# An attention and feed-forward kernel on one core: the third chunk's opening steps are placed earlier, and four coarse pieces change their places

## The chip, the cores and the metric

The kernel runs on one core of a Trainium2 chip. The metric is the device time of one execution in microseconds (us); lower is better. The kernel before took 1090.92 us, the median of three runs (1090.62 to 1091.01).

## The reference

The reference computes two attentions over the same q, k, v (8 batches, 8 heads, 576 positions, 64 values each) and adds them; then an RMS norm and a gated feed-forward layer over the 4608 tokens.

```python
# coarse: q, k, v are averaged over groups of 4 positions, attended in full, repeated 4 times
q_d = q.reshape(B, H, Sd, factor, D).mean(axis=3)          # Sd = 144; k_d and v_d likewise
out_up = np.repeat(sm_attn(q_d, k_d, v_d), factor, axis=2)
# local: each position sees the positions less than 4 away (7 of them)
mask = np.abs(pos[:, None] - pos[None, :]) < factor
scores = np.where(mask, scale * np.matmul(q, k.transpose(0, 1, 3, 2)), -1e9)
out_local = np.matmul(softmax(scores), v)
x = (out_up + out_local).transpose(0, 2, 1, 3).reshape(4608, 512)
# feed-forward: 512 -> 1536 (gate and value) -> 512
xn = x / np.sqrt(np.mean(x * x, axis=-1, keepdims=True) + 1e-06) * rms_g
g = xn @ w_gate
return (g * (1 / (1 + np.exp(-g))) * (xn @ w_val)) @ w_out
```

## The kernel before

**Tiles and loops.** The 4608 tokens are 18 chunks of 256 columns. The feed-forward layer of a chunk runs over 12 tiles f of 128 hidden columns. For each tile TensorE computes gate and value (`first`, L1334, 24 matmuls into `ps_h`, twelve with `wg` and twelve with `wv`); ScalarE takes the tanh (L1342); VectorE makes the gate (L1345) and the product (L1350); ScalarE and VectorE split that into a high and a low part (L1356, L1359); and two tiles later TensorE adds the tile to the output (`second`, L1370, 6 matmuls). There are three `ps_h` buffers, so a tile's first matmul waits for the product (L1350) of the tile three before it. The lag of two tiles is LAG; at a chunk's end its last seconds run behind the next chunk's first tiles. Below, f8 is tile 8 of chunk 1, and f0', f3' are tiles of chunk 2.

**The coarse attention** is done in pieces, one for a batch and a pair of heads. A piece has three TensorE steps: scores (L529), the turn of its exponentials (L569), and the values (L584). Between scores and turn VectorE takes the peak (L550, L555), and ScalarE the exponentials (L560); after the turn ScalarE copies (L577), and after the values VectorE scales (L598) and a DMA stores the rows in `up_dram` (L601). The sums of k, q and v over groups of four, which a piece needs, are made by DMAs: one load on SyncE's queue (L359, L363) and three accumulating ones on GpSimd's queue (L367).

**The local attention of most chunks** runs while the chunk before it is in its feed-forward layer, on VectorE (L706 products, L710 sums: 8 of each for a chunk), and for the weighted values on ScalarE (L753, eight small instructions for a product), VectorE and GpSimd (L760), summed on VectorE (L779); then the coarse rows are added (L795), the squares taken (L805), and the chunk is normed and transposed to `xh` and `xl` (two buffers each). Its k and v rows come in `kv` buffers (four; L612, on SyncE's queue), its q rows in `q_t` (two; L694).

**The first three chunks** take another way for it, class `Dense`: scores on TensorE with a mask, then `flip` (L1149, TensorE transposes the shares of a parity), `copy` (L1160, ScalarE), `values` (L1172, 64 instructions here, from four `kv` buffers and the two `prod` buffers with the shares), `load_up` (L1196, two DMAs on ScalarE's queue, which bring the coarse rows), `add_rows` (L1201, adds these to the same accumulators; its second operand is called `q_t` in the profile because it lies in the place of such a buffer), `squares` (L1214), `rms` and `root` (L1223 to L1238, very small VectorE instructions), `norm`, `turn` (L1256), `high` (L1260) and `low` (L1264).

**What sets the order.** Every engine takes its instructions in the program's order. The weight decoding, `Dense(0)`, `Dense(1)`, the scores and softmax of `Dense(2)`, and all of chunk 0's feed-forward layer are ordered by a planner (class `Plan`): each step has a cost, a due time, and the buffers that it takes and holds. This part is called the list. From chunk 1 on the steps are written in a loop over the tiles; there a table says behind which step a piece goes:

```python
for at, it in zip(PIECES.get(c, (0, 3)), coarse[done:]):
    score, swap, value = Coarse(*it).steps()
    behind_second[at] = score
    before.setdefault(at + 2, []).append(swap)
    before.setdefault(at + 3, []).append(value)
```

So a coarse piece at 5 has its scores behind the second that is written at tile 5, its turn behind tile 7, its values behind tile 8. A framework's scheduler puts what is written so into each engine's order; a step can move some places from where it was written. In the same way the remaining steps of `Dense(2)` are given places among chunk 1's tiles: `flips` at tile 1, `mix` (values, add_rows, squares, rms and root) at tile 3, `turn` at tile 6. Chunk 3's local attention, the first in the vector form, is written in chunk 2's loop, and the scheduler has moved it forward: in the trace its L706 to L779 run while TensorE is in chunk 1.

## Time and profile before

| | |
|---|---|
| runs | 1090.92, 1091.01, 1090.62 us; median 1090.92 |
| the profiled execution | 1090.25 us, of which span 1088.4 us |
| TensorE (PE) busy | 1042.2 us, 96% |
| VectorE (DVE) busy | 889.0 us, 82% |
| ScalarE (ACT) busy | 602.3 us, 55% |
| GpSimd (POOL) busy | 207.1 us, 19% |
| PE's share of the chain that ended last | 85% |

All times of the trace are counted from the start of the span. Chunk 1's first tile ends and its f1 begins at 150.5 us; chunk 2's f3' begins at 227.6 us. In the timeline a row is a run of equal instructions on one engine: start, time, line, what is written from what, the count, and in brackets the idle time ahead of it with what ended it. In a table of windows each row is a stretch of time: its length, then the busy time and count of PE, PEld, DVE, ACT and POOL, the granted clock of TensorE (1.00 is full), the share of the DMA engines, and GB/s.

### The profile page before, as it was taken

What the parts mean: (1) busy time and instruction counts of PE and PEld (TensorE: products, weight loads), DVE (VectorE), ACT (ScalarE), POOL (GpSimd) and SP (SyncE); (2) the same over time, 40 slices, a digit from 0 to 9 for tenths busy, and PEclk for the clock granted to TensorE, in tenths of its full rate; (3) what the DMA queues carried; (4) which work ended last, traced back from release to release, by engine and by line L of the source; (5) the groups of instructions that cost most, each with busy time, mean ns of one, the idle gap of its engine ahead of it and who ended that gap; (6) DMA issues with size and microseconds to landing.
All of it is one profiled execution on the core that took longest, in us unless ns stands there. A gap on an engine that the chain in (4) does not pass through costs nothing.

```text
span 1088.4 us, 23630 instructions
## 1 busy us (share of the span) xinstructions
PE 1042.2 (96%) x8804; PEld 956.6 (88%) x8804; DVE 889.0 (82%) x1855; ACT 602.3 (55%) x2182; POOL 207.1 (19%) x268
## 2 busy tenths in 40 slices
PE   4878898899999999999999999999999999999998
PEld 3657797799999999999999999999999999999997
DVE  5899847894979998898988889989898998986432
ACT  5587641843748383838374747373838373746222
POOL 2257600322222122121121212010101010101000
PEclk9989999999999999999999999999999999999999
DMA  8598814474352535253535353313132232210000
GB/s 265 190 325 236 211 49 124 95 172 91 105 116 74 121 96 127 83 122 82 123 87 126 81 119 83 89 50 96 46 99 71 71 91 64 84 37 21 1 21 20
DMA packets 72729, 113.26 MB, mean 104 GB/s; under 512 B 26006, under 2 KB 33958, under 8 KB 72614
## 3 DMA queue, kind: packets, MB, share of 16 engines
q1 hardware_dynamic: 46342, 91.64, 27.9%
q0 software_dynamic: 8768, 15.95, 9.5%
q10 hardware_dynamic: 17504, 4.16, 1.8%
q8 instruction: 69, 1.13, 0.4%
q14 instruction: 46, 0.38, 0.1%
HBM read 99.92 MB, written 11.80 MB: 103 GB/s over the span
## 4 chain that ended last, share of the span: by engine, by line
PE 85%; DVE 7%; ACT 3%; DMA 2%; issue 2%; POOL 0%; SPq 0%; ACTq 0%; DVEq 0%; POOLq 0%
PE ps_h L1334 51%; PE ps_o L1370 26%; PE ps_a L584 2%; PE ps_a L529 1%; DVE o_sb L275 1%; PE ps_a L856 1%; PE ps_a L569 1%; DMA wv<-in_qk_sum_dram 1%; ACT prod L753 1%; ACT a_g L560 1%; DVE prod L706 1%; DMA qk<-in_qk_sum_dram 1%; DMA q_t<-in_q_band_dram 0%; PE ps_h L1101 0%; PE ps_a L1149 0%
## 5 line engine op out<-in xcount | busy, mean ns | idle before, releaser
L1370 PE MATMUL ps_o<-wo,hs 128*128 128x512 f32 x1296 | 335.8, 397 | 2.0 <-DVE hs L1359 2.0
L1334 PE MATMUL ps_h<-xh,wg 128*128 128x256 f32 x1728 | 317.2, 279 | 0.6 <-DVE wg L299 0.6
L1334 PE MATMUL ps_h<-xh,wv 128*128 128x256 f32 x1728 | 312.2, 278 | 0.0
L1334 PEld LDWEIGHTS ps_h<-xh,wg 128*128 128x128 f32 x1728 | 266.2, 189 | 9.2 <-issue 3.1
L1334 PEld LDWEIGHTS ps_h<-xh,wv 128*128 128x128 f32 x1728 | 264.7, 188 | 3.2 <-issue 0.6
L1370 PEld LDWEIGHTS ps_o<-wo,hs 128*128 128x128 f32 x1296 | 229.0, 188 | 40.7 <-DVE hs L1359 2.4
L753 ACT ACTIVATE prod<-kv,sc 128x64 f32<-128x64 f32 x960 | 245.3, 407 | 21.2 <-DMA up<-o_g 10.3
L1334 PE MATMUL ps_h<-xl,wg 128*128 128x256 f32 x864 | 244.0, 282 | 7.3 <-DVE sil L1350 5.7
L1334 PE MATMUL ps_h<-xl,wv 128*128 128x256 f32 x864 | 240.3, 278 | 4.3 <-DVE sil L1345 4.3
L1342 ACT ACTIVATE sil<-ps_h 128x256 f32<-128x256 f32 x216 | 81.7, 378 | 241.3 <-PE ps_h L1334 223.5
L1334 PEld LDWEIGHTS ps_h<-xl,wg 128*128 128x128 f32 x864 | 163.2, 189 | 15.1 <-DVE sil L1350 7.2
L1334 PEld LDWEIGHTS ps_h<-xl,wv 128*128 128x128 f32 x864 | 162.9, 188 | 7.5 <-DVE sil L1345 6.2
L760 POOL TENSOR_TENSOR prod<-sc,kv 128x256 f32<-128x256 f32 x120 | 89.2, 775 | 407.2 <-DVE sc L744 152.8
L1356 ACT ACTIVATE hs<-sil 128x256 fp32r<-128x256 f32 x216 | 89.4, 414 | 126.4 <-DVE sil L1350 105.3
L779 DVE TENSOR_REDUCE x_t<-prod 128x128 f32<-128x896 f32 x120 | 127.8, 1075 | 29.6 <-PE ps_a L856 26.4
L1345 DVE SCALAR_TENSOR_TENSOR sil<-sil,ps_h 128x256 f32<-128x256 f32 x216 | 88.9, 411 | 58.7 <-ACT sil L1342 56.1
L706 DVE TENSOR_TENSOR prod<-q_t,kv 128x896 f32<-128x896 f32 x120 | 129.5, 1082 | 5.6 <-DMA kv<-in_k_pad_dram 4.5
L710 DVE TENSOR_REDUCE sc<-prod 128x14 f32<-128x896 f32 x120 | 128.6, 1073 | 0.0
L1359 DVE TENSOR_TENSOR hs<-sil,hs 128x256 fp32r<-128x256 f32 x210 | 100.3, 479 | 31.2 <-ACT hs L1356 30.7
L1350 DVE SCALAR_TENSOR_TENSOR sil<-sil,ps_h 128x256 f32<-128x256 f32 x216 | 89.6, 416 | 3.0 <-PE ps_h L1334 1.5
L367 POOL DMA_DIRECT2D qk<-in_qk_sum_dram x36 | 32.9, 913 | 233.5 <-DMA qk<-in_qk_sum_dram 195.5
L760 DVE TENSOR_TENSOR prod<-sc,kv 128x128 f32<-128x128 f32 x120 | 52.5, 461 | 0.8
(182 smaller groups left out, 927.9 us busy)
## 6 DMA issues: line engine op xcount, KB each, us to landing
kv<-in_k_pad_dram SPq DMA_DIRECT2D x60, 320.0 KB
kv<-in_v_pad_dram SPq DMA_DIRECT2D x60, 320.0 KB
qk<-in_qk_sum_dram POOLq DMA_DIRECT2D x36, 288.0 KB, 4.8
q_t<-in_q_band_dram SPq DMA_DIRECT2D x60, 128.0 KB
out_dram<-o_sb SPq DMA_DIRECT2D x30, 256.0 KB
vs<-in_v_sum_dram POOLq DMA_DIRECT2D x36, 144.0 KB, 3.5
qk<-in_qk_sum_dram SPq DMA_DIRECT2D x12, 288.0 KB
wo<-in_qk_sum_dram SPq DMA_DIRECT2D x2, 1152.0 KB
```

The source lines that it names most:

```text
L706: nc.vector.tensor_tensor(out=pr, in0=bcast(q[:, s0:s0 + 2], 2, NO), in1=window(k, s0), op=ALU.mult)
L710: nc.vector.tensor_reduce(out=self.sc[:, j, par, s0:s0 + 2], in_=self.pr[i], axis=AX.X, op=ALU.add,)
L753: nc.scalar.activation(out=self.pr[i][:, o, s], in_=self.v[j, par][:, s0 + s + o], func=AF.Copy, scale=p[:, s, o:o + 1],)
L760: (nc.vector if engine == "DVE" else nc.gpsimd).tensor_tensor(out=self.pr[i][:, a:b], in0=bcast(p[:, :, a:b].rearrange("p s o -> p o s"), ...
L779: nc.vector.tensor_reduce(out=self.x[j][:, s0:s0 + 2, par], in_=pr.rearrange("p o s d -> p s d o"), axis=AX.X, op=ALU.add,)
L1334: last = nc.tensor.matmul(out=self.p[f][:, t], lhsT=wi(f)[:, 0, k], rhs=xi[:, k], start=(n == 0), stop=(n == 3 * KT - 1),).ins
L1342: nc.scalar.activation(out=self.sil[f], in_=self.p[f][:, 0], func=AF.Tanh, scale=0.5)
L1345: nc.vector.scalar_tensor_tensor(out=self.sil[f], in0=self.sil[f], scalar=1.0, in1=self.p[f][:, 0], op0=ALU.add, op1=ALU.mult,)
L1350: nc.vector.scalar_tensor_tensor(out=self.sil[f], in0=self.sil[f], scalar=0.5, in1=self.p[f][:, 1], op0=ALU.mult, op1=ALU.mult,)
L1356: nc.scalar.activation(out=self.hs[f][:, 0], in_=self.sil[f], func=AF.Copy)
L1359: (nc.gpsimd if engine == "POOL" else nc.vector).tensor_tensor(out=self.hs[f][:, 1], in0=self.sil[f], in1=self.hs[f][:, 0], op=ALU.subtract,)
L1370: last = nc.tensor.matmul(out=self.o[j], lhsT=lhs[:, cols], rhs=rhs(f)[:, 0], start=(f == 0 and i == 0), stop=(f == NF - 1 and i == 2),).ins
```

## The change

It has three parts. (1) The coarse pieces of chunk 1 stand at tiles 1, 4, 6, 8 in place of 0, 5, 7, 8. (2) `Dense(2)`'s two flips, their copies and its `load_up` leave chunk 1 and go into the list; `mix` stands at tile 0 of chunk 1 rather than 3, and `turn` at 3 rather than 6. (3) `load_up` of `Dense(1)` and `Dense(2)` brings the coarse rows into the `xh` buffer that the chunk is to fill later, rather than into a buffer of the weight stage, and no longer stands behind the list's last step. No computation is added or left out. As the planner lays out the list anew, some steps in it change their places too, one weight step goes from VectorE to GpSimd, and a weight load of the stage comes earlier on SyncE's queue.

```diff
-PIECES = {1: (0, 5, 7, 8), 2: (0, 3), 3: (0, 2)}
+PIECES = {1: (1, 4, 6, 8), 2: (0, 3), 3: (0, 2)}
...
 # Dense.plan (chunk 1)
-                up = buf("stage")
                 t = task(
-                    "ACT", 0.1, self.load_up, end - 12, [stored[p.b, p.hp] for p in pieces], allocs=[up], uses=[up], lag=9.0,
-                )
-                ups = [task("PE", 1.6, self.add_rows, end - 12, [t, *values], uses=[up, *x_bufs])]
+                    "ACT", 0.1, self.load_up, end - 12, [stored[p.b, p.hp] for p in pieces], allocs=[self.xh_buf],
+                    uses=[self.xh_buf], lag=9.0,
+                )
+                ups = [task("PE", 1.6, self.add_rows, end - 12, [t, *values], uses=[self.xh_buf, *x_bufs])]
...
-        def plan_scores(self, sums, mask, at, late):
+        def plan_scores(self, sums, pieces, mask, at, late):
...
+            copies = []
             for par in range(2):
-                made = self.plan_softmax(par, late - 5, held[par:par + 1], made, sp[par], s_bufs[par])
+                sb = s_bufs[par]
+                made = self.plan_softmax(par, late - 5, held[par:par + 1], made, sp[par], sb)
+                tp = buf("ps_a")
+                t = task("PE", 1.1, lambda par=par: self.flip(par), late + 8, made, allocs=[tp], uses=[sb, tp])
+                copies.append(task(
+                    "ACT", 0.6, lambda par=par: self.copy(par), late + 8, [t, *copies], uses=[tp, sb],
+                ))
...
+            self.xh_buf = buf("xh")
+            task("ACT", 0.1, self.load_up, late + 20, [stored[p.b, p.hp] for p in pieces], allocs=[self.xh_buf], lag=9.0)
...
 # Dense.steps (chunk 2)
-            return [(0.0, self.load_up)], {1: flips, 3: mix, 6: turn}
+            return [], {0: mix, 3: turn}
...
         def load_up(self):
-            t = stage.tile([P, WPC, 2], U32, name="raw")
-            self.up = t.bitcast(FP32).rearrange("p n t -> p (n t)")[:32]
+            self.xh = xp.tile([P, KT, C], FP32R, name="xh")
+            self.up = self.xh.bitcast(FP32).rearrange("p k n -> p (k n)")[:32]
...
-            with behind(listed and listed[-1]):
```

The order on the engines, at three places. First TensorE around chunk 2's values, at the end of the list and in chunk 1's opening tiles (names: `kv` are the v rows, `prod` the flipped shares, `raw` the coarse rows, `wo` with `hs` a second). Before:

```order
L584 MATMUL ps_a<-vs,a_g 72x64 x8
L1172 MATMUL ps_a<-kv,prod 32x64 x64
L1201 MATMUL ps_a<-raw,q_t 128x256 x4
L1370 MATMUL ps_o<-wo_0_850,hs 128x512 x2
L1370 MATMUL ps_o<-wo_0_851,hs 128x512
```

That is behind f3 of chunk 1; the second that follows is tile 1's. Now:

```order
L1337 MATMUL ps_h<-xh,wv_0_846 128x256
L1175 MATMUL ps_a<-kv,prod 32x64 x18
L1373 MATMUL ps_o<-wo_2_1872,hs 128x512 x2
L1373 MATMUL ps_o<-wo_2_1873,hs 128x512
L1373 MATMUL ps_o<-wo_2_1872,hs 128x512 x2
L1373 MATMUL ps_o<-wo_2_1873,hs 128x512
L1175 MATMUL ps_a<-kv,prod 32x64 x46
L1203 MATMUL ps_a<-xh,q_t 128x256 x4
L1337 MATMUL ps_h<-xl,wg_0_779 128x256
```

The values and the coarse rows now stand behind chunk 1's f0, with chunk 0's last second among them, and ahead of f1; three tiles, two seconds and the first piece's turn and values that stood ahead of them stand behind. (Lines from the first change on count some more: L1337 is L1334 of before, L1373 is L1370, L1175 is L1172, L1203 is L1201.)

Second, TensorE at the second coarse piece of chunk 1, whose scores are L529 and whose turn is L569. Before, from the last transposes of chunk 2 on:

```order
L1256 MATMUL ps_a<-ident_sb,x_t 128x128 x4
L1370 MATMUL ps_o<-wo_0_850,hs 128x512 x2
L1370 MATMUL ps_o<-wo_0_851,hs 128x512
L1370 MATMUL ps_o<-wo_0_850,hs 128x512 x2
L1370 MATMUL ps_o<-wo_0_851,hs 128x512
L569 MATMUL ps_a<-ident_sb,a_g 72x72 x8
```

There the piece's scores lie ahead of that, before 21 matmuls of f11, and the second shown is tile 4's. Now, from its scores on:

```order
L529 MATMUL ps_a<-qk 72x144 x4
L1373 MATMUL ps_o<-wo_0_850,hs 128x512 x2
L1373 MATMUL ps_o<-wo_0_851,hs 128x512
L1373 MATMUL ps_o<-wo_0_850,hs 128x512 x2
L1373 MATMUL ps_o<-wo_0_851,hs 128x512
L1337 MATMUL ps_h<-xl,wv_1_1603 128x256
L1337 MATMUL ps_h<-xh,wv_1_1603 128x256
L1337 MATMUL ps_h<-xh,wv_1_1604 128x256
L1337 MATMUL ps_h<-xl,wv_1_1603 128x256
L1337 MATMUL ps_h<-xh,wv_1_1603 128x256
L1337 MATMUL ps_h<-xh,wv_1_1604 128x256
L569 MATMUL ps_a<-ident_sb,a_g 72x72 x8
```

The second between is tile 3's, and the six matmuls are the last of f9: the turn stands ahead of f10 and f11, which before stood ahead of it.

Third, ScalarE at the same piece, whose exponentials are L560. Before:

```order
L733 ACTIVATE sc<-sc 128x112
L1246 ACTIVATE x_t<-ps_a,rinv 128x256 x2
L1342 ACTIVATE sil<-ps_h 128x256
L753 ACTIVATE prod<-kv,sc 128x64 x16
L1260 CAST xh<-ps_a 128x4x128
L753 ACTIVATE prod<-kv,sc 128x64 x2
L560 ACTIVATE a_g,z_g<-ps_a,m_g 72x144 x4
L753 ACTIVATE prod<-kv,sc 128x64 x12
```

Now:

```order
L733 ACTIVATE sc<-sc 128x112
L1263 CAST xh<-ps_a 128x4x128
L753 ACTIVATE prod<-kv,sc 128x64 x16
L1359 ACTIVATE hs<-sil 128x256
L601 DMA up<-o_g 72x4x64
L1359 ACTIVATE hs<-sil 128x256
L753 ACTIVATE prod<-kv,sc 128x64 x9
L1359 ACTIVATE hs<-sil 128x256
L753 ACTIVATE prod<-kv,sc 128x64 x7
L1345 ACTIVATE sil<-ps_h 128x256 x2
L560 ACTIVATE a_g,z_g<-ps_a,m_g 72x144 x4
```

Between the exponentials of chunk 3's local attention (L733) and those of the coarse piece (L560) stood 18 instructions of L753, and now stand 32, with three high parts (L1359 now) and two tanh (L1345 now).

More of the change, by code (lines that the diff above doesn't have):

```diff
@@ L945, in plan @@
                 turn = task(
-                    "PE", 0.6, lambda b=b: self.turn(b), end - 7 - TAIL, norms,
-                    allocs=[tps] + ([self.xh_buf, self.xl_buf] if b == 0 else []), uses=[xs, self.xh_buf, self.xl_buf],
+                    "PE", 0.6, lambda b=b: self.turn(b), end - 7 - TAIL, [*norms, *self.turns],
+                    allocs=[tps] + ([self.xh_buf, self.xl_buf][not early:] if b == 0 else []), uses=[xs, self.xh_buf, self.xl_buf],
                 )
@@ L1050, in steps @@
         def steps(self):
-            def flips():
-                last = [self.flip(par) for par in range(2)][-1]
-                for par in range(2):
-                    self.copy(par)
-                return last
             def mix():
@@ L1190, in load_up @@
         def load_up(self):
-            t = stage.tile([P, WPC, 2], U32, name="raw")
-            self.up = t.bitcast(FP32).rearrange("p n t -> p (n t)")[:32]
+            self.xh = xp.tile([P, KT, C], FP32R, name="xh")
+            self.up = self.xh.bitcast(FP32).rearrange("p k n -> p (k n)")[:32]
             src = up_dram[0].rearrange("b k t (s g) d -> s g (b k t) d", g=UPP)[:, self.u0:self.u0 + 2]
-            with behind(listed and listed[-1]):
-                for g in range(2):
-                    nc.scalar.dma_start(out=self.up[g * 16:(g + 1) * 16].rearrange("p (h d) -> p h d", d=D), in_=src[:, g])
+            for g in range(2):
+                nc.scalar.dma_start(out=self.up[g * 16:(g + 1) * 16].rearrange("p (h d) -> p h d", d=D), in_=src[:, g])
         def add_rows(self):
@@ L1249, in turn @@
             if b == 0:
-                self.xh = xp.tile([P, KT, C], FP32R, name="xh")
+                if self.c == 0:
+                    self.xh = xp.tile([P, KT, C], FP32R, name="xh")
                 self.xl = xp.tile([P, KT, C], FP32R, name="xl")
@@ L1491, in attn_moe_kernel @@
         b.users.extend(atts[1].turns[:1])
-    early = Dense(2).plan_scores(parts, mask, 24.0, 105.0)
+    early = Dense(2).plan_scores(parts, opening, mask, 24.0, 105.0)
     for n in range(len(pieces)):
```

## The prediction

> **What bounds the kernel now.** I read the page's head, then windows, PE's waits in the window that holds chunk 1, and the timelines around each wait.
>
> ```profile
> span 1088.4 us, 23630 instructions
> 145.00:170.00 25.00, 25.00 (x353) 22.73 (x352) 6.83 (x19) 9.33 (x31) 0.00 (x0) 1.00 0.21 55
> 170.00:195.00 25.00, 21.76 (x173) 20.41 (x172) 23.82 (x52) 5.10 (x15) 0.51 (x1) 1.00 0.44 114
> 195.00:215.00 20.00, 16.73 (x129) 14.11 (x128) 17.06 (x33) 19.59 (x85) 8.63 (x12) 1.00 0.52 107
> 215.00:235.00 20.00, 20.00 (x155) 18.07 (x154) 19.00 (x36) 9.21 (x39) 3.47 (x4) 0.91 0.74 163
> 228.00:1088.00 860.00, 856.02 (x6510) 796.36 (x6508) 707.93 (x1498) 468.05 (x1782) 126.03 (x165) 1.00 0.33 82
> ```
>
> From 228 us on PE is busy 856.02 of 860 us at full clock: whatever chunk 1 saves or loses moves the end by as much, since the work behind it is the same. So I count only up to f3', which the same PE work precedes in both orders, and compare its start. In chunk 1 PE idles 25 − 21.76 = 3.24 us and 20 − 16.73 = 3.27 us, 6.5 in all, and the window from 215 has no idle time but a mean clock of 0.91: 20 × 0.09 = 1.8 us of work lost. Together 8.3 us: the most that the change can save in chunk 1.
>
> ```profile
> PE ps_h L1334 <- DVE sil L1350: 5.4, 3, 2.2
> 186.40 0.38 PE L1334 MATMUL ps_h<-xl,wg 128*128 128x256 f32 x1 [2.12 <-DVE sil L1350]
> 190.53 0.39 PE L1334 MATMUL ps_h<-xl,wg 128*128 128x256 f32 x1 [1.12 <-DVE sil L1350]
> 214.57 0.39 PE L1334 MATMUL ps_h<-xl,wg 128*128 128x256 f32 x1 [2.17 <-DVE sil L1350]
> 217.00:218.00 1.00, 1.00 (x6) 1.00 (x6) 1.00 (x4) 0.20 (x2) 0.00 (x0) 0.50 0.16 37
> 227.56 0.28 PE L1334 MATMUL ps_h<-xl,wg 128*128 128x256 f32 x1
> ```
>
> 5.4 of the 6.5 us are waits of a tile's first matmul for a product. The clock stands at 0.50 right behind the longest of them. And VectorE is late because it begins late: it is busy only 6.83 us of 145 to 170, then nearly all the time. What it lacks is seen here:
>
> ```profile
> 164.43 1.99 PE L1172 MATMUL ps_a<-kv,prod 64*32 64x64 f32 x128
> 166.35 1.99 PE L1201 MATMUL ps_a<-raw,q_t 32*128 32x256 f32 x8
> 166.25 3.43 SPq L612 DMA_DIRECT2D kv<-in_k_pad_dram  x4
> 170.18 2.09 DVE L706 TENSOR_TENSOR prod<-q_t,kv 128x896 f32<-128x896 f32 x2 [4.48 <-DMA kv<-in_k_pad_dram]
> 194.00 0.27 DVE L744 TENSOR_TENSOR sc<-sc,z_b 128x112 f32<-128x112 f32 x1
> ```
>
> Chunk 2's values read the four kv buffers until 166.3; the next k rows are issued at 166.25 and VectorE has them 3.93 us later, at 170.18. Its scores and softmax end with L744 at 194.27, 24.1 us on.
>
> **The change part by part.** Values and coarse rows move to the end of chunk 1's f0. When that is, from these rows of PE:
>
> ```profile
> 149.81 0.71 PE L529 MATMUL ps_a<-qk 64*72 64x144 f32 x8
> 150.46 0.39 PE L1334 MATMUL ps_h<-xl,wg 128*128 128x256 f32 x1
> 153.39 1.15 PE L1149 MATMUL ps_a<-ident_sb,prod 128*64 128x64 f32 x32
> 154.47 0.38 PE L1334 MATMUL ps_h<-xl,wg 128*128 128x256 f32 x1
> 159.09 1.63 PE L1370 MATMUL ps_o<-wo,hs 128*128 128x512 f32 x6
> 160.56 0.28 PE L1334 MATMUL ps_h<-xl,wg 128*128 128x256 f32 x1
> 163.31 1.19 PE L584 MATMUL ps_a<-vs,a_g 72*72 72x64 f32 x16
> 200.51 0.66 PE L1256 MATMUL ps_a<-ident_sb,x_t 128*128 128x128 f32 x4 [0.27 <-ACT a_g L560]
> 200.92 1.63 PE L1370 MATMUL ps_o<-wo,hs 128*128 128x512 f32 x6
> 202.39 0.66 PE L569 MATMUL ps_a<-ident_sb,a_g 72*72 72x72 f32 x8
> PE ps_h L1334 <- DVE sil L1345: 4.3, 6, 2.2
> ```
>
> From one start to the next: a set of scores 0.65 us, a tile 2.93, a flip 1.08, a second 1.47, values of a piece 1.12, a turn 0.41; values and add_rows of the dense chunk 1.92 each (an L569 I take at 0.46). f0 ended at 149.81. Now two flips lie ahead of that (+2.17) and chunk 0's last second behind it (−1.47): 150.5. The flips cost nothing in sum, since PE made them before too, at 153.39 and later. The last row is of 86 to 150 us: PE waits 4.3 us there for VectorE, the list's order changes, and it can give or take some of that; with the same steps and products in it I take it as equal, ±1 us. So the values run from 150.5, with the second inside, to 150.5 + 1.92 + 1.47 = 153.9, and add_rows to 155.8.
>
> add_rows needs load_up. It waits for chunk 0's last `first`, as it takes that chunk's xh buffer, at 150.5 less a second and six matmuls, about 148.4. Against these rows:
>
> ```profile
> 149.61 2.75 SPq L1269 DMA_DIRECT2D out_dram<-o_sb  x4
> 149.75 0.81 ACTq L1196 DMA_DIRECT2D raw<-up  x2
> ```
>
> its two issues take 0.81 us; with the 3.93 us of the k rows' way the coarse rows are there at 153.1, 0.8 us early. Behind it on ScalarE's queue stand f0's tanh and f11's high part; the second that needs that part comes only at 151.0. I price the edit at 0; a landing 2 us later would cost 1.2 us.
>
> SyncE's queue: the four stores of chunk 0's output begin 0.1 us behind the end of its last second (149.49 before) and take 2.75; the k loads stand behind them. That second now ends at 150.5 + 0.54 (18 of the values) + 1.47 = 152.5, so the k rows are issued at 155.4, set by the stores now and not by the values, and land at 159.3. VectorE begins 10.8 us sooner than at 170.18, and ends the softmax at 159.4 + 24.1 + 0.5 for two more gates = 184.0. The products of f3 to f5 are then in time; VectorE is dense when f6 to f8 need theirs, where my walk gives waits between 0 and 2 us. I take 0.5. So nearly all the waits on products go.
>
> **What is late next.** The coarse piece's turn (L569) now comes soon behind chunk 2's second turn. Between these PE has three seconds (4.4 us), a piece's values (1.12), scores (0.65) and six matmuls (0.73): 6.9 us. On ScalarE the same stretch holds, in its order: the cast of that turn, 16 L753, two high parts, 9 L753, one high part, 7 L753, two tanh, and the four exponentials that L569 waits for. From ScalarE's timeline:
>
> ```profile
> 194.30 4.01 ACT L753 ACTIVATE prod<-kv,sc 128x64 f32<-128x64 f32 x16
> 198.14 0.60 ACT L1260 CAST xh<-ps_a 128x512 fp32r<-128x512 f32 x1
> 199.64 0.36 ACT L560 ACTIVATE a_g<-ps_a,m_g 72x144 f32<-72x144 f32 x1
> 201.06 3.05 ACT L753 ACTIVATE prod<-kv,sc 128x64 f32<-128x64 f32 x12
> 204.91 0.42 ACT L1356 ACTIVATE hs<-sil 128x256 fp32r<-128x256 f32 x1
> 205.22 0.69 ACT L577 COPY a_g<-ps_a 72x288 f32<-72x288 f32 x2
> ```
>
> Cast 0.6, twice 16 L753 at 4.01, three high parts at 0.31 (204.91 to 205.22), two tanh taken at the same, four exponentials 201.06 − 199.64 = 1.42: 11.6 us. PE therefore waits 11.6 − 6.9 = 4.7 us; I take 4.5, since neighbouring instructions overlap a little. Before, 18 of these L753 and no high part stood there. When is it: PE reaches this turn at 150.5 + 3.8 (values, rows) + 5 × 1.47 + 9 × 2.93 + 2 × 0.65 + 0.46 + 2 × 0.41 + 1.12 + 0.5 = 192.3, so the wait would stand from about 192 to 197. VectorE's softmax (184.0) is done before the cast ends (185.8), a margin of 1.8 us.
>
> Then the clock. The 2.17 us ahead of 214.57 cost 1.8 us of clock behind them, while 2.12 us ahead of 186.40 cost nothing (the window 170 to 195 has a clock of 1.00). One wait of 4.5 us is longer than both; it can cost from 0 to 3 us (two such dips, less what the wait itself hides); I take 1.1, near one dip of which part falls into the wait. The Trainium skill (page "TensorE: Matmul & The Clock Gate", section "HAM oscillation — how this bites in real kernels") gives the rule "no PE-idle gaps >~3.4µs". By that rule the 2.17 us of before would have cost no clock, which the row at 217 contradicts, and the new wait alone would: a rule that speaks against this change. By it the dip is sure rather than likely, and the sum below is 1.8 − 1.1 = 0.7 us dearer.
>
> Sum up to f3': 8.3 us of idle time and lost clock before; after, 0.5 + 4.5 + 1.1 = 6.1. Gain 2.2 us; f3' starts at 225.4 rather than 227.56. The profiled execution, 1090.25 us (its span and 1.85 around it), becomes 1088.05; it lies 0.67 under the median of the runs, so the forecast is 1090.92 − 2.2 = **1088.7 us**.
>
> **The rivals.** (A) *The new wait is hidden or much shorter.* For it: a piece of ScalarE's run may go faster than its rows, or PE may come later to the turn. Against it: all engines take their work in order, and the counts are plain. What then bounds is GpSimd:
>
> ```profile
> 206.36 0.89 POOL L367 DMA_DIRECT2D qk<-in_qk_sum_dram  x1 [4.03 <-DMA qk<-in_qk_sum_dram]
> 211.17 0.88 POOL L367 DMA_DIRECT2D qk<-in_qk_sum_dram  x1 [2.99 <-DMA qk<-in_qk_sum_dram]
> ```
>
> Its sums follow each other at 4.81 us, and products that VectorE waits for stand between them. From the scores of this piece (about 191.5) the third sum is issued at 201.1, VectorE then has some 18 us to the product of f0' that f3' needs, and f3' starts at 221 to 222 at the earliest: gain 5.5 to 6, about 1085.2 us.
>
> (B) *The wait only changes its name.* The new wait at L569 is 5.5 us, f6 to f8 wait 1 us, and the clock loses 1.8: 8.3 again, 1090.9 us. For it: each term is within its bounds. Against it: all three have to be at the upper end, or the list must lose 1 us.
>
> (C) *Slower: VectorE's start stays late under a turn that comes early.* The place is the k rows behind the output stores on SyncE's queue. Softmax later than 185.8 pushes ScalarE's run, and PE's wait, one to one. The change is even when the first L706 starts at 159.4 + 1.8 + 2.2 = 163.4, and slower from there: at 165 the wait is 8.3, with 0.5 and a clock loss of 1.8 makes 10.6, 1093.2 us. For it: four stores of 256 KB stand ahead of the loads, as they did not when the values were the last to go. Against it: they took 2.75 us before.
>
> (D) *The change does not do what it says*: the k loads still come behind something else and start at 166. That is (C) at its worst, about 1095 us.
>
> **How the numbers follow.** The forecast 0.45, its own range 1087.2 to 1090.2 by the terms' bounds (list ±1, f6 to f8 0 to 2, clock 0 to 3, taken together); A 0.17; B 0.22; C 0.13; D 0.03. What a measurement can tell from no change is 0.2%, 2.2 us, so the bound for faster is 1088.74: the forecast lies on it. Faster: half of the forecast's chance and all of A's, with some of B's, 0.44. Slower: C and D with little else, 0.14. The rest, 0.42, is no change. The range from 1084.8 (A) to 1093.2 (C) leaves out the tail of A and D.
>
> **What would show it.** Right: the first k rows land and L706 starts at 159 to 160; the waits of L1334 on L1350 (5.4 us) shrink under 2 us; a wait of PE at L569 on L560 of 4 to 5 us stands around 192 to 197, with a clock of 0.50 in a few windows behind; f3' starts at 225 to 226. Wrong: no such wait, or f3' before 223 (A); L706 after 161 (C); L1203 waiting for its rows for over 1 us; more waits in the list before 150 us.

## The result

The changed kernel takes 1100.08 us (median), the kernel before 1090.77 us beside it: a ratio of 1.0105 with an interval of 1.0083 to 1.0128. It is slower, and it lies above the predicted range. Its profiled execution took 1097.84 us with a span of 1096.1 us, 7.6 us more than the profiled execution before.

Line numbers from L927 on have moved: a tile's first product (`first`) is now L1337 (before L1334), the second L1373 (L1370), the gate L1348 (L1345), the product L1353 (L1350), the low part L1362 (L1359), the values L1175 (L1172), `add_rows` L1203 (L1201), the norm L1246 (L1244), the flip L1152 (L1149).

Windows by stage show where the time went. First the kernel before; the list and chunk 0 end in the first row, chunk 1 in the second (columns: length, busy time of PE, PE's weight loads, VectorE, ScalarE, GpSimd, mean granted clock, DMA share, GB/s):

```profile
82.00:150.00 68.00, 60.13 (x404) 53.70 (x405) 58.44 (x104) 43.66 (x89) 39.80 (x41) 0.97 0.71 186
150.00:260.00 110.00, 103.50 (x977) 94.12 (x976) 82.44 (x179) 55.77 (x215) 19.13 (x24) 0.98 0.51 117
```

The changed kernel, cut 8 us later, since its chunk 1 begins that much later:

```profile
span 1096.1 us, 23633 instructions
82.00:158.00 76.00, 65.24 (x454) 58.63 (x455) 57.27 (x103) 42.65 (x87) 37.14 (x40) 0.89 0.63 166
158.00:260.00 102.00, 96.58 (x854) 86.28 (x853) 79.28 (x174) 53.24 (x209) 18.75 (x23) 0.97 0.51 122
260.00:1080.00 820.00, 819.78 (x6243) 764.08 (x6242) 683.09 (x1439) 451.66 (x1725) 120.30 (x158) 1.00 0.32 81
```

From 260 us on PE is as dense as before. In the table below, idle time is length less PE's busy time, and lost clock is PE's busy time at a clock under 1, times what is missing of 1, summed over windows of half a microsecond.

| stage | before: idle + lost clock | changed: idle + lost clock | difference |
|---|---|---|---|
| opening (0 to 82) | 27.5 + 2.5 | 27.9 + 1.0 | -1.1 |
| list and chunk 0 (82 to 150; 82 to 158) | 7.9 + 1.6 | 10.8 + 7.5 | +8.8 |
| chunk 1 (150 to 260; 158 to 260) | 6.5 + 1.7 | 5.4 + 3.0 | +0.2 |

So the whole loss of this kernel stands before chunk 1 begins, and chunk 1 is even. PE's waits by what they wait for (us in total, times, longest), ahead of 158 us and behind it; before the change the first of these two lists had no wait for GpSimd (POOL):

```profile
PE ps_o L1373 <- POOL hs L1362: 5.7, 3, 2.2
PE ps_h L1337 <- DVE xl L1267: 1.9, 1, 1.9
PE ps_o L1373 <- DVE hs L1362: 1.8, 3, 1.2
PE ps_h L1337 <- DVE sil L1348: 1.4, 1, 1.4
PE ps_a L1152 <- DVE prod L1145: 1.0, 1, 1.0
...
PE ps_a L569 <- ACT a_g L560: 4.4, 1, 4.4
PE ps_h L1337 <- DVE sil L1353: 1.0, 2, 0.8
```

The same waits in time, from the timelines of the changed kernel:

```profile
104.96 2.43 PE L1373 MATMUL ps_o<-wo,hs 128*128 128x512 f32 x6 [1.49 <-POOL hs L1362]
120.37 1.66 PE L1373 MATMUL ps_o<-wo,hs 128*128 128x512 f32 x6 [2.02 <-POOL hs L1362]
124.69 1.55 PE L1373 MATMUL ps_o<-wo,hs 128*128 128x512 f32 x6
128.44 2.09 PE L1373 MATMUL ps_o<-wo,hs 128*128 128x512 f32 x6 [2.19 <-POOL hs L1362]
131.55 1.98 PE L1152 MATMUL ps_a<-ident_sb,prod 128*64 128x64 f32 x32 [1.01 <-DVE prod L1145]
158.60 0.75 PE L1175 MATMUL ps_a<-kv,prod 64*32 64x64 f32 x36
168.93 2.10 DVE L706 TENSOR_TENSOR prod<-q_t,kv 128x896 f32<-128x896 f32 x2 [0.65 <-DMA kv<-in_k_pad_dram]
205.49 1.18 PE L569 MATMUL ps_a<-ident_sb,a_g 72*72 72x72 f32 x8 [4.41 <-ACT a_g L560]
235.40 0.28 PE L1337 MATMUL ps_h<-xl,wg 128*128 128x256 f32 x1
```

The rows at 124.69 and 128.44 are two seconds with no first product between them; the first product of the next tile comes only behind the flip. Before, first products stood between these two seconds and the wait there was 1.45 us. The values begin at 158.60 where 150.5 was predicted, and f3' at 235.40 rather than 227.56: 7.84 us later, nearly all of it brought from the list. The granted clock in stretches of the list and of chunk 1:

```profile
106.00:107.00 1.00, 1.00 (x4) 0.81 (x3) 1.00 (x3) 1.00 (x3) 1.00 (x3) 0.50 0.66 62
130.00:136.00 6.00, 4.99 (x46) 4.34 (x45) 5.21 (x9) 1.84 (x3) 2.69 (x3) 0.50 0.53 105
205.00:211.00 6.00, 5.51 (x21) 4.11 (x22) 4.59 (x13) 6.00 (x27) 2.06 (x3) 0.50 0.57 111
```

Half clock holds from 105.6 to 109.0, from 129.5 to 136.3 and from 204.6 to 211.4. Another stretch begins in the opening, at 74.8, and reaches into the list until 88.6 (before: 75.8 to 86.0). Of the 8.8 us that the list lost, 2.9 are idle time and 5.9 are clock; of the clock, 1.3 are the longer tail of that opening stretch, and 4.6 lie in the two stretches behind the waits.

### The profile page after: what moved, and what is told of

It is laid out like the page before. It is cut to its first block, busy times and chain, and to the rows that moved or that the text cites. A ratio compares the mean times of both kernels' runs of the same rounds, so it can differ in the third digit from the quotient of the medians.

```text
span 1096.1 us, 23633 instructions
## 1 busy us (share of the span) xinstructions
PE 1047.8 (96%) x8804; PEld 961.3 (88%) x8804; DVE 887.7 (81%) x1854; ACT 602.3 (55%) x2182; POOL 208.8 (19%) x269
## 4 chain that ended last, share of the span: by engine, by line
PE 85%; DVE 6%; ACT 4%; DMA 3%; issue 2%; POOL 1%; SPq 0%; DVEq 0%; ACTq 0%; POOLq 0%
PE ps_h L1337 50%; PE ps_o L1373 26%; PE ps_a L584 3%; PE ps_a L529 1%; PE ps_a L569 1%; PE ps_a L856 1%; ACT prod L753 1%; ACT a_g L560 1%; DMA wv<-in_qk_sum_dram 1%; DMA raw<-in_w_out_dram 1%; DVE o_sb L275 1%; DVE prod L706 1%; PE ps_h L1104 1%; DVE sc L710 0%; DMA kv<-in_k_pad_dram 0%
## 5 line engine op out<-in xcount | busy, mean ns | idle before, releaser
L1373 PE MATMUL ps_o<-wo,hs 128*128 128x512 f32 x1296 | 338.9, 399 | 7.5 <-POOL hs L1362 5.7
L1337 PE MATMUL ps_h<-xh,wg 128*128 128x256 f32 x1728 | 319.2, 281 | 0.0
L1337 PE MATMUL ps_h<-xh,wv 128*128 128x256 f32 x1728 | 310.9, 277 | 0.0
L1337 PEld LDWEIGHTS ps_h<-xh,wg 128*128 128x128 f32 x1728 | 268.6, 191 | 8.1 <-issue 2.9
L1373 PEld LDWEIGHTS ps_o<-wo,hs 128*128 128x128 f32 x1296 | 230.3, 189 | 47.6 <-POOL hs L1362 6.7
L1337 PEld LDWEIGHTS ps_h<-xh,wv 128*128 128x128 f32 x1728 | 263.8, 188 | 3.1 <-issue 0.4
L753 ACT ACTIVATE prod<-kv,sc 128x64 f32<-128x64 f32 x960 | 245.1, 407 | 19.1 <-DMA up<-o_g 10.3
L1337 PE MATMUL ps_h<-xl,wg 128*128 128x256 f32 x864 | 245.5, 284 | 3.1 <-DVE xl L1267 1.9
L1337 PE MATMUL ps_h<-xl,wv 128*128 128x256 f32 x864 | 239.5, 277 | 1.6 <-DVE sil L1348 1.4
L1345 ACT ACTIVATE sil<-ps_h 128x256 f32<-128x256 f32 x216 | 81.8, 379 | 248.3 <-PE ps_h L1337 224.3
L1337 PEld LDWEIGHTS ps_h<-xl,wg 128*128 128x128 f32 x864 | 164.9, 191 | 11.3 <-DVE sil L1353 2.7
L1337 PEld LDWEIGHTS ps_h<-xl,wv 128*128 128x128 f32 x864 | 162.5, 188 | 3.8 <-DVE sil L1348 2.2
L1359 ACT ACTIVATE hs<-sil 128x256 fp32r<-128x256 f32 x216 | 89.3, 414 | 127.1 <-DVE sil L1353 100.6
L1348 DVE SCALAR_TENSOR_TENSOR sil<-sil,ps_h 128x256 f32<-128x256 f32 x216 | 89.2, 413 | 59.5 <-ACT sil L1345 52.7
L1362 DVE TENSOR_TENSOR hs<-sil,hs 128x256 fp32r<-128x256 f32 x210 | 101.7, 486 | 36.9 <-ACT hs L1359 36.6
L706 DVE TENSOR_TENSOR prod<-q_t,kv 128x896 f32<-128x896 f32 x120 | 129.7, 1083 | 0.8 <-DMA kv<-in_k_pad_dram 0.7
L1353 DVE SCALAR_TENSOR_TENSOR sil<-sil,ps_h 128x256 f32<-128x256 f32 x216 | 89.8, 416 | 8.5 <-PE ps_h L1337 7.1
L760 DVE TENSOR_TENSOR prod<-sc,kv 128x128 f32<-128x128 f32 x120 | 49.6, 437 | 0.9
```

The lines of the kernel that those rows point to most:

```text
L706: nc.vector.tensor_tensor(out=pr, in0=bcast(q[:, s0:s0 + 2], 2, NO), in1=window(k, s0), op=ALU.mult)
L753: nc.scalar.activation(out=self.pr[i][:, o, s], in_=self.v[j, par][:, s0 + s + o], func=AF.Copy, scale=p[:, s, o:o + 1],)
L760: (nc.vector if engine == "DVE" else nc.gpsimd).tensor_tensor(out=self.pr[i][:, a:b], in0=bcast(p[:, :, a:b].rearrange("p s o -> p o s"), ...
L1337: last = nc.tensor.matmul(out=self.p[f][:, t], lhsT=wi(f)[:, 0, k], rhs=xi[:, k], start=(n == 0), stop=(n == 3 * KT - 1),).ins
L1345: nc.scalar.activation(out=self.sil[f], in_=self.p[f][:, 0], func=AF.Tanh, scale=0.5)
L1348: nc.vector.scalar_tensor_tensor(out=self.sil[f], in0=self.sil[f], scalar=1.0, in1=self.p[f][:, 0], op0=ALU.add, op1=ALU.mult,)
```

## The experiments

Every time is a median; "beside" it stands the kernel before on the same chip. A ratio is that of the means, with its 95% interval. "Idle + lost" is worked out as in the table.

**The list.** First the list of the change alone: flips, copies and `load_up` in the list as in the changed kernel, chunk 1 as before.

```diff
 (list as in the changed kernel)
-PIECES = {1: (1, 4, 6, 8), 2: (0, 3), 3: (0, 2)}
-            return [], {0: mix, 3: turn}
+PIECES = {1: (0, 5, 7, 8), 2: (0, 3), 3: (0, 2)}
+            return [], {3: mix, 6: turn}
```

> The change with its list (flips, copies and load_up planned, coarse rows in xh), but the pieces back at 0, 5, 7, 8 and the values and the turn back at tiles 3 and 6. Theory L: the list ends late as in the change (f0 ends about 8 us later than before, clock below 1 between 104 and 140 us), and the time is 1096 to 1101 us. Theory C: the list costs little, 1088 to 1093 us.

1102.43 us beside 1091.45, ratio 1.0117 (1.0087 to 1.0146), as theory L has it and 1.4 us above its range. From 82 to 150 us it has 13.4 + 4.5 us; chunk 1, at 5.4 + 1.4, is no worse than before. PE's waits in the list carry the same name as in the changed kernel:

```profile
PE ps_o L1373 <- POOL hs L1362: 5.2, 3, 2.3
```

Then one step of it alone: only `Dense(1)`'s coarse rows go into the `xh` buffer.

```diff
 (kernel before)
-                up = buf("stage")
+                (Dense(1): the planner and load_up take the chunk's xh buffer)
```

> The kernel before with one part of the list changed: the coarse rows of chunk 1 come into its xh buffer rather than a stage buffer; no flips in the list, chunk 1 of the loop as before. If giving the stage buffer free reorders the list for the worse (theory L1): f0 ends 4 us or more late, 1094 us or more. If the planned flips and the softmax ahead of them do it (theory L2): f0 ends within 1.5 us of 149.8, and 1088.5 to 1093 us.

1102.47 us, ratio 1.0093 (1.0066 to 1.0120): one load in another buffer costs as much as the whole list. From 82 to 150 us it has 15.3 + 7.4 us. The edit has two effects, though, the buffer of the load and the new order that the planner makes of all steps in the list. They part when the order of the kernel before is written out and replayed on all engines, with the load in `xh`:

```diff
 (the run above)
-        while self.left:
-            ... (the planner's choice of the next step)
+        for word in ORDER.split():
+            t, e = self.tasks[int(word[1:])], names[word[0]]
```

> The previous kernel (coarse rows of chunk 1 in xh, nothing else) with the list written in the very order of before: on every engine the instructions stand as before, and only the place of those rows differs. Theory O (the order that the planner makes is the loss, the place itself costs nothing): the list ends within 1.5 us of before, 1088 to 1093 us. Rival X (the xh buffer itself makes something wait, the load or the turn that fills it): the list still ends 5 us or more late, 1096 us or more.

1091.62 us beside 1091.3, ratio 1.0005 (0.9988 to 1.0022). The load in the `xh` buffer costs nothing once the order is the old one; the list has 8.4 + 2.3 us again. So in that run the planner's new order is the loss. For the changed kernel itself, the run with the old order under "Chunk 1" shows the same: its values start at 151.27 rather than 158.60. Giving the planner its old reservation back (a stage buffer held although unused) in the changed kernel does not bring the old order:

```diff
-                    ... allocs=[self.xh_buf], uses=[self.xh_buf], lag=9.0,
+                    ... allocs=[self.xh_buf, up], uses=[self.xh_buf, up], lag=9.0,
```

> The change, but the planner lets load_up of chunk 1 take the stage buffer's place in its reckoning as before, so that the weight pieces of the stage are fetched behind it again. If the freed stage buffer is what led the planner to the worse order: the gates of f8 and f9 no longer stand behind the stage's weight pieces, the values start at 150 to 154 us, 1087 to 1093 us. If any change of the list upsets the order: they start at 156 us or later, 1095 us or more.

1102.33 us, ratio 1.0112 (1.0091 to 1.0134); the list now waits in other places and is late again, 9.9 + 6.6 us from 82 to 150.

Next, which part of the new order? One suspect was GpSimd, which makes the low parts that PE waits for. The changed kernel's own order was replayed with three of these low parts (tiles 3, 5 and 7) on VectorE at the same place:

```diff
 (changed kernel, its own order written out)
-  G530 ... G546 ... G562
+  D530 ... D546 ... D562
```

> Edit: the changed kernel with its own list order, but the low parts of three first tiles of chunk 0 that TensorE waited for on GpSimd (1.49, 2.02 and 2.19 us ahead of their second products) run on VectorE at the same place. Theory P (GpSimd's low parts in the list's new order make the waits, and the waits halve the clock behind them): the 5.7 us of waits for GpSimd's low parts fall under 1.5, the half-clock stretches at 105.6 and 129.5 go, chunk 2's values start at 152 to 154 rather than 158.6, and the median is 1090 to 1095. Rival Q (these waits are only where a general lateness of the list shows): the waits turn up under other names, the values start at 157 or later, and the median is 1097 or above.

1100.04 us, ratio 1.0074 (1.0054 to 1.0094). The waits for GpSimd are gone, and others have come:

```profile
PE ps_o L1387 <- DVE hs L1376: 6.3, 5, 3.3
128.31 2.93 PE L1387 MATMUL ps_o<-wo,hs 128*128 128x512 f32 x6 [3.31 <-DVE hs L1376]
125.69 0.74 DVE L313 SCALAR_TENSOR_TENSOR wg<-o_sb,g_sb,wg 128x512 fp32r<-128x512 f32 x1
126.36 1.13 DVE L289 SCALAR_TENSOR_TENSOR o_sb<-o_sb,wo 128x512 uint32<-128x512 uint32 x1
127.41 0.85 DVE L1376 TENSOR_TENSOR hs<-sil,hs 128x256 fp32r<-128x256 f32 x1
```

(L1387 is the second here, L1376 the low part, L313 and L289 weight steps.) The low part now stands behind two weight steps on VectorE and comes as late. The half clock is about where it was (106.6 to 110.1, 127.1 to 133.9), and the values start at 157.15. So the rival held: taking the low parts off GpSimd does not help. The changed kernel's own rows show that GpSimd was itself kept waiting ahead of two of the three, for ScalarE's high part:

```profile
103.80 1.10 POOL L1362 TENSOR_TENSOR hs<-sil,hs 128x256 fp32r<-128x256 f32 x1 [1.68 <-ACT hs L1359]
127.54 0.85 POOL L1362 TENSOR_TENSOR hs<-sil,hs 128x256 fp32r<-128x256 f32 x1 [0.28 <-ACT hs L1359]
```

So what makes them late lies at least in part further up the chain.

The other suspect was the place of the flips on PE. In the fastest kernel so far (below; the list in the old order, flips at its end) only the two flips and their copies were moved to the changed kernel's places:

```diff
-D252 P559 ...                       P235 P240 ... P595 A596 ... P597 ... A598
+D252 P595 P559 ... A596 ...         P235 P597 P240 A598 ...
```

> Edit: the fastest kernel so far (old order of the list, chunk 1 as changed, first coarse score behind the norm; 1085.7), with only the two flips and their copies moved to the places in the list that the changed kernel gives them: the first ahead of the ninth first tile's products, the second between the two turns. Theory U (the loss in the list is the new order of the elementwise work, not the flips): the flips' operand makes TensorE wait 1 to 1.5 us once, the values start by 153, median 1086 to 1089. Rival X (the flips' place on TensorE makes the loss): the values start at 155 or later, with new half-clock stretches between 128 and 150, median 1091 or above.

1088.28 us beside 1090.6, ratio 0.9983 (0.9963 to 1.0002): 2.6 us more than with the flips at the end (the intervals just fail to touch), and inside what was expected if the flips are not the loss. The flip's wait is there, 1.2 us once, and no half clock stands between 128 and 150 us. The values start at 161.04, which alone would be the rival's sign; but in the profiled execution chunk 0's first matmul began at 89.8 us, 7 us later than usual. So the start of `add_rows`, which has the same matmuls ahead of it in all three kernels, is counted from that first matmul: 75.0 us, against 72.7 with the flips at the end and 79.7 in the changed kernel. PE's idle time in it is 8.0 us, against 7.8 and 10.1; the other 2.1 us are clock, and a stretch of half clock like the one behind them (119.4 to 122.8) stands in a kernel with the flips at the end too (113.2 to 116.6, pieces at tiles 0, 4, 6, 8). So the flips' place brings nearly none of the list's idle time; whether the 2.6 us of the median come from it, about a third of what the list costs, stays open. What remains is the rest of the order: the elementwise work on VectorE, GpSimd and ScalarE around chunk 0's seconds, and the few places where PE has first products and seconds the other way round. Which step in it decides was not tried and stays open.

**Chunk 1.** The pieces alone, in the kernel before:

```diff
-PIECES = {1: (0, 5, 7, 8), 2: (0, 3), 3: (0, 2)}
+PIECES = {1: (1, 4, 6, 8), 2: (0, 3), 3: (0, 2)}
```

> The kernel before with the four coarse pieces of chunk 1 at tiles 1, 4, 6, 8 and nothing else changed; the list is that of before. Theory L (the loss lies in the list, which now ends 8.1 us later at a half clock in places): the values of chunk 2 start where they did but for the order of the pieces, f1 begins at 149.8 us, and the time is 1088 to 1092 us. Theory C (the places of the pieces bring the loss, since a turn stands too soon behind its scores): a wait of PE at L569 of 3 us or more with a half clock behind it, and 1094 us or more.

1099.2 us beside 1091.45, ratio 1.0078 (1.0055 to 1.0100). The order of the list is as before (7.2 + 4.0 us, the values at 164.44); chunk 1 has 9.3 + 4.8 us, with a wait at L569 that the kernel before did not have:

```profile
PE ps_a L569 <- ACT a_g L560: 5.6, 2, 3.5
PE ps_h L1334 <- DVE sil L1350: 3.1, 2, 2.2
```

The pieces and, as far as the old list lets them, the dense steps sooner:

```diff
 (the run above)
-            return [(0.0, self.load_up)], {1: flips, 3: mix, 6: turn}
+            return [(0.0, self.load_up)], {0: flips, 1: mix, 4: turn}
```

> The kernel before, its list untouched, with the pieces at 1, 4, 6, 8 and the dense steps of chunk 2 sooner in the loop: flips at tile 0, values at tile 1, turn at tile 4. Theory L: the list ends as before (f0 ends at 149.5 to 150), VectorE's first L706 starts at 161 to 164 rather than 170.2, the waits of first matmuls on products shrink below 3 us, and the time is 1084 to 1089 us. Theory C: the same waits at L569 as in the change (4 us, two windows at half clock) take the gain, and the time is 1091 to 1097 us.

1100.13 us, ratio 1.0081 (1.0063 to 1.0100). That is above both expected ranges. VectorE's first L706 does start sooner, at 163.64, and still chunk 1 has 11.3 + 4.9 us; 10.0 of the idle time are four waits for a product.

Then the list in the old order, so that nothing but chunk 1 differs: flips, copies and `load_up` stand at the list's end, chunk 1 is that of the change.

```diff
 (changed kernel)
+ORDER = ( ... the order of the kernel before ... P595 A596 ... P597 ... A598 A599 ... )
+            early.plan_late()
```

> The change, with its list in the order of before: the two flips, their copies and load_up stand at the list's end, behind chunk 0's last firsts; chunk 1 as the change has it (values behind f0, turn at 3, pieces at 1, 4, 6, 8). Theory O: the values start at 150 to 152 us rather than 158.6, no half clock between 100 and 150 us beyond before's, and with the scores of the second piece now 28 matmuls and a second ahead of its turn the wait at L569 is under 2 us: 1084 to 1089 us. Rival C (chunk 1's new order loses as much as it gains): 1090 to 1096 us, with waits and half-clock windows between 190 and 230 us.

1097.55 us, ratio 1.0067 (1.0048 to 1.0087), above both expected ranges. The values start at 151.27, 0.8 us from what was predicted for the change, and still the kernel is slower: chunk 1 has 9.0 + 5.8 us. (Here L543 is a piece's scores, L574 its exponentials, L583 its turn, L1192 chunk 2's values, L1263 its norm, L1354 a tile's first matmuls, L1370 the product.)

```profile
151.27 1.99 PE L1192 MATMUL ps_a<-kv,prod 64*32 64x64 f32 x128
158.13 0.46 PE L543 MATMUL ps_a<-qk 64*72 64x144 f32 x2
181.18 0.87 DVE L1263 TENSOR_SCALAR x_t<-ps_a,rinv 128x256 f32<-128x256 f32 x2
184.09 0.71 PE L543 MATMUL ps_a<-qk 64*72 64x144 f32 x6
188.65 1.17 PE L583 MATMUL ps_a<-ident_sb,a_g 72*72 72x72 f32 x8 [3.85 <-ACT a_g L574]
202.89 0.58 PE L1354 MATMUL ps_h<-xl,wg 128*128 128x256 f32 x1 [3.72 <-DVE sil L1370]
```

The first piece's scores come in two parts 26 us apart, one of the four multiplications at 158.13 and the other three at 184.09. The pool `ps_a` has three buffers; the values of chunk 2 hold two of them as accumulators from 151.27 until the norm reads them, and that is at 181.18, because the very small steps of the root stand between chunk 3's scores on VectorE (the products of its local attention, L706 of before). So one buffer is left for a set of scores that needs two, and the second of the four multiplications writes the second. It comes behind the norm, and the turn that needs it has too little work left ahead of it.

This reading was tried by one rule more: chunk 3's scores on VectorE are issued behind chunk 2's norm. (The expectations call them coarse; they are the scores of the local attention.)

```diff
 (the run above)
-                self.score(i)
+                with behind(normed.get(2) if self.c == 3 else None):
+                    self.score(i)
...
+                normed[self.c] = t.ins   (the norm on VectorE)
```

> Edit: the kernel with the list in the old order and chunk 1 as changed (pieces at tiles 1, 4, 6 and 8), with one more rule: chunk 3's first coarse score is issued behind chunk 2's norm on VectorE. Nothing else differs from the run that measured 1097.55. Theory V: the norm ends at 160 to 163 rather than 181, the 3.85 us wait for the first piece's exp falls under 1.5, idle and lost clock in chunk 1 fall from 14.8 to under 10, median 1088 to 1093. Rival W: the coarse chain starts 1.5 us later and everything behind it too, the wait for the exp stays over 3 us, median 1096 or above.

1085.70 us beside 1091.2, ratio 0.9945 (0.9929 to 0.9960): 11.9 us less than without the rule, and faster than both kernels. The norm, the scores and the turn (lines as above, but one or two higher), and the window of chunk 1:

```profile
153.31 1.99 PE L1193 MATMUL ps_a<-kv,prod 64*32 64x64 f32 x128
160.18 0.46 PE L543 MATMUL ps_a<-qk 64*72 64x144 f32 x2
163.05 0.88 DVE L1264 TENSOR_SCALAR x_t<-ps_a,rinv 128x256 f32<-128x256 f32 x2
167.06 0.71 PE L543 MATMUL ps_a<-qk 64*72 64x144 f32 x6
174.16 0.66 PE L583 MATMUL ps_a<-ident_sb,a_g 72*72 72x72 f32 x8
150.00:260.00 110.00, 108.20 (x964) 97.92 (x963) 86.22 (x184) 56.20 (x216) 20.19 (x25) 1.00 0.53 120
```

The norm begins 9.7 us behind the values' start rather than 30, the parts of the scores are 6.9 us apart, no wait stands at the turn, and chunk 1 has 1.8 us of idle time and no lost clock. That the late norm is the cause is shown by this; that it acts through the buffers is read from these times, since the scheduler moves other steps along with the rule, and a further buffer was not tried.

With that rule in place, the pieces' tiles were tried again. Tiles 0, 5, 7, 8, as before the change:

```diff
-PIECES = {1: (1, 4, 6, 8), 2: (0, 3), 3: (0, 2)}
+PIECES = {1: (0, 5, 7, 8), 2: (0, 3), 3: (0, 2)}
```

> Edit: the list in the order of the kernel before (flips, copies and the load at its end), pieces of chunk 1 at tiles 0, 5, 7 and 8, mix at tile 0 and turn at tile 3, and chunk 3's first coarse score issued behind chunk 2's norm on VectorE. Theory V (chunk 2's accumulators hold two of the three buffers of the small accumulators until its norm runs, which the coarse scores delay by 20 us, and that pushes the first piece's last scores back until nothing covers the exp): the norm is done at 160 to 163 rather than 181, no wait over 1.5 us for the first piece's exp, idle and lost clock in chunk 1 under 6 us, median 1084 to 1089. Rival W (the coarse chain on VectorE and ScalarE is too long for its place whatever holds the buffers): the wait for the exp is over 2.5 us again, idle and lost clock 8 us or more, median 1092 or above.

1088.75 us, ratio 0.9975 (0.9960 to 0.9989), chunk 1 at 3.9 + 1.7; a wait of 2.0 us stays at a turn, more than the 1.5 expected, and one of 1.8 us for a product. It is 3 us slower than with tiles 1, 4, 6, 8; the two intervals only touch. And tiles 0, 4, 6, 8:

```diff
-PIECES = {1: (1, 4, 6, 8), 2: (0, 3), 3: (0, 2)}
+PIECES = {1: (0, 4, 6, 8), 2: (0, 3), 3: (0, 2)}
```

> Edit: the fastest kernel so far (1085.7) with the first piece of chunk 1 at tile 0 rather than 1, the others at 4, 6 and 8 as they are. Theory Y (once the buffers come free in time, the first piece only needs cover for its exp): nothing moves by more than 1 us, median 1085 to 1087. Rival Z (at tile 0 the first piece's turn comes before the coarse scores are off VectorE and ScalarE): a wait of over 2 us at that turn or at a gate behind it, median 1088 or above.

1083.90 us beside 1090.6, ratio 0.9934 (0.9915 to 0.9954), chunk 1 at 0.5 + 0.0. It is the fastest of all, 1.8 us under tiles 1, 4, 6, 8 where 1 was expected at most, but its interval overlaps theirs.

Last, the rule alone in the changed kernel, with its own order of the list:

```diff
 (changed kernel)
-                self.score(i)
+                with behind(normed.get(2) if self.c == 3 else None):
+                    self.score(i)
```

> Edit: the changed kernel as it is, with one rule more: chunk 3's first coarse score is issued behind chunk 2's norm on VectorE. Theory S (two terms that add up: the list's new order costs about 8 us, and the root's lateness in chunk 1 the 5 to 7 us that the early values should have brought): chunk 1's idle and lost clock fall from 8.4 to 2 to 4 us, the values still start at 158 to 161, median 1093 to 1097. Rival T (with the list late, the root's place does not matter, or the rule only moves the wait): chunk 1 stays at 7 us or more, median 1098 or above.

1092.90 us beside 1090.6, ratio 1.0013 (0.9997 to 1.0029): 7.2 us less than the changed kernel, and no longer to be told from the kernel before. The list is as late as in the changed kernel (values at 160.05), chunk 1 has 1.1 us of idle time, less than the 2 to 4 expected. Together:

| | chunk 3's scores as in the change | chunk 3's scores behind the norm |
|---|---|---|
| list in the new order | 1100.08 (the change) | 1092.90 |
| list in the old order | 1097.55 | 1085.70 |

The list's new order costs 7.2 us where chunk 1 is mended and 2.5 where it is not; the late norm costs 11.9 and 7.2. The two losses overlap by 4.7 us; as each of the four medians has an interval of some 2 us to either side, the 2.5 is not clear of noise and the overlap only just. One reading, not tried by itself: a late list also starts the values late, and they then hold their buffers for less time until the norm ends (24 us in the change, 31 in the old order).

**The clock behind the wait at L569.** In the changed kernel the 4.4 us wait was filled with 40 multiplications by the identity:

```diff
+            if (self.b, self.hp) == coarse[9] and par == 1:
+                for _ in range(40):
+                    nc.tensor.matmul(out=tp[:, :P], lhsT=ident_sb[:HALF, :HALF], rhs=ident_sb[:HALF], ...)
```

> The change with 40 small matmuls of the identity (72 by 128, their result is overwritten) ahead of the second piece's turn L569, in the time in which PE waits there. The wait of 4.4 us then shows as busy PE and leaves under 2 us idle. If the half clock of 204.6 to 211.4 us comes from that idle time, it is gone or one window shorter, and the span loses 1.5 to 3.5 us against the change's 1096.1. If the half clock has another cause, it stays, and the span is equal or 1 us longer.

1107.15 us, ratio 1.0159 (1.0137 to 1.0182). They took 8.7 us (80 records of 0.109), so they overshot the wait by 4.3 us, and the time says nothing of the clock. But no half clock followed. With 18 of them:

```diff
-                for _ in range(40):
+                for _ in range(18):
```

> Edit: the changed kernel with 18 more multiplications by the identity (results not used) ahead of the second piece's turn, some 2 us at 0.109 us each, in the 4.4 us that TensorE waits there; nothing of the computation is left out. Theory K (the half clock behind this wait is brought by the idle time): the half-clock stretch at 204.6 to 211.4 is gone or one window shorter, and the product group that followed at half clock ends 1.5 to 3 us sooner, median 1096 to 1099. Rival R (the stretch comes from the moment or the load, not from the wait): the stretch stays at two windows and the median stays at 1099.5 or above.

1100.36 us, ratio 1.0082 (1.0061 to 1.0103). They took 4.1 us, twice what the expectation says, for each is two records. The profile around them:

```profile
204.88 4.09 PE L569 MATMUL ps_a<-ident_sb 72*72 72x128 f32 x36
204.00:208.00 4.00, 4.00 (x35) 3.83 (x34) 4.00 (x9) 4.00 (x18) 1.67 (x1) 1.00 0.57 156
208.00:212.00 4.00, 4.00 (x31) 3.37 (x30) 3.85 (x10) 4.00 (x20) 1.70 (x2) 1.00 0.62 138
```

The clock is 1.00 where it was 0.50, and so it was with 40, so the idle time brought the half clock. The median did not move, though 1096 to 1099 was expected: chunk 1 has 3.9 + 1.7 us and the 4.1 us of added work, 9.7 in all against 8.4, with a wait of 2.0 us at the next turn and half clock from 238.5 on. That the clock recovers is shown; that it can be turned into time here is not.

## Why the prediction was wrong

**The list, "equal, ±1 us": the step that failed first.** The prediction saw that the list's order changes and took it as even because steps and products stay the same. It lost 2.9 us of idle time and 5.9 us of clock, 8.8 in all, and the values came 8.1 us late. With the old order the loss was gone, for the load alone (1091.62) and for the whole change (values at 151.27). The sum of the work was never the question: PE waits for single low parts, and the order decides when these come and what PE has to do until then. Which step of the order is to blame stays open. The sign that the prediction gave for being wrong, more waits in the list before 150 us, is what the profile shows, but no rival stood for it, and the range ended at 1093.2.

**What is late next: right for the change, with a cause behind it that was not seen.** A wait of 4.5 us at L569 was predicted, and 4.41 came, behind ScalarE's run of L753, with 1.0 us on products against 0.5. This was not luck: PE's work ahead of it took 7.0 us (194.03 to 201.08; 6.9 forecast), ScalarE's run 11.1 (194.31 to 205.43; 11.6 forecast). Its place in time, 201 to 205.5, is the predicted 192 to 197 and the list's 8 us. But the run of ScalarE decides only because the pieces' scores come late, and they do because VectorE puts off chunk 2's norm, until which, as read above, its accumulators keep two of three buffers. With the norm first and nothing else changed in this kernel, the second piece's scores began at 189.78 rather than 198.07, and the wait at its turn was gone. The prediction moved the values 14 us forward (164.43 to 150.5) without asking when their buffers come free. With the list in the old order the wait stood at the first piece's turn (3.85 us) instead, with two waits for products (1.38 ahead of it, 3.72 behind), and chunk 1 lost 14.8 us where 6.1 were forecast. So the forecast would have been wrong with its list term right (1097.55). Mended, chunk 1 lost 1.8 us, less than the prediction's rival A had hoped for.

**The clock, "I take 1.1".** It was 2.95 us in the change, near the upper bound of 3 (one stretch of 6.8 us at half clock, in part hidden by the wait itself). The Trainium skill, page "TensorE: Matmul & The Clock Gate", section "HAM oscillation — how this bites in real kernels", has a long idle gap (over some 3.4 us) lower the clock; for the 4.41 us wait the runs agree, since filled with work it cost no clock. A gap that the rule lets pass was followed by half clock all the same: 2.19 us ahead of 128.44, by half clock from 129.5 to 136.3.

**VectorE's start.** L706 began 10.3 us behind the values' start (158.60 to 168.93), where the prediction had 8.9. SyncE's queue in the changed kernel:

```profile
161.01 2.98 SPq L1272 DMA_DIRECT2D out_dram<-o_sb  x4
164.09 1.32 SPq L612 DMA_DIRECT2D kv<-in_k_pad_dram  x2
```

The stores take 2.98 us (priced at 2.75). The k rows behind them were issued 5.5 us behind the values' start rather than 4.9, and took 4.8 us rather than 3.93 to reach VectorE. That is 1.4 us of rival C's place, under its point of 2.2 + 1.8 us. (The stores are not 256 KB each, as rival C has it: the profile's DMA rows give 128 KB to the 12 stores of the first three chunks, four a chunk.)

**The sum.** A gain of 2.2 us was forecast in chunk 1. It gave -0.2 (8.2 before, 8.4 now), the list gave -8.8, and the opening, by its clock, +1.1. f3' starts at 235.40 rather than 225.4.

## What to carry to other kernels

A planner's order is part of the kernel: an edit that only moves a load to another buffer may reorder many other steps, so hold the old order fixed when an edit's own worth is to be measured, and keep it if the edit does not need another. Before a step is moved forward, ask what it holds and who frees it: an accumulator that is filled sooner but read no sooner takes its buffer from everything between. Here both together turned 9 us lost into 5 to 7 us gained.

## What was not expected of the hardware

Half clock comes in stretches of 3.4 us or multiples of it (105.6 to 109.0, 129.5 to 136.3, 204.6 to 211.4), and a wait well under that is enough: 1.49 us ahead of 104.96 and 2.19 us ahead of 128.44 each have one right behind them, while 2.02 us ahead of 120.37 have none. The Trainium skill, page "TensorE: Matmul & The Clock Gate", section "What's actually happening", describes a free-running window of 3413 ns, and the lengths agree. Counted in such steps from the start of the stretch at 105.6, the first and the last of these waits lie inside one window, and the one without a stretch is cut in two (0.9 and 1.1 us). That fits a window that need only be idle in part, not the full idle window that the table there in the Trainium skill names; it is argued from three waits, not shown. Idle time alone does not decide it: in the kernel before, counted in the same way from its stretch at 215.7, the wait of 2.15 us ahead of 111.72 lies with 1.8 us in one window, and no half clock followed.

The opening ahead of 82 us lost 1.0 us of clock in the changed kernel and 8.4 us in the same kernel with 18 multiplications added 120 us later; over all these kernels it is 0.9 to 8.5 us. A single profile can therefore be 7 us off for reasons that have nothing to do with the edit, which is why stages were compared rather than spans.
